# Attention backward for one query row: finer first and last loads, dK of pair 0 ahead of pair 1's K blocks, and O written out sooner

## The chip, the cores and the metric

The kernel runs on one NeuronCore of a Trainium2 chip. Its engines each run their own list of instructions in order: TensorE (PE in the profile, with PEld for its weight loads), VectorE (DVE), ScalarE (ACT), GpSimd (POOL) and SyncE (SP), which here only issues DMAs. One list of DMAs issued by SP is worked off by sixteen DMA engines; every transfer is cut over all sixteen. The metric is the device time of one execution in microseconds. The kernel before takes 647.64 us (median of 3 runs, 647.38 to 647.68).

## The reference: what is computed

Thirty-two heads, one query row each, 8192 keys, head size 128, all in bf16. The outputs are O and the gradients of q, k and v for a given dO:

```
scores = einsum('bhqd,bhkd->bhqk', q, k) * Dh**-0.5      # q [1,32,1,128], k, v [1,32,8192,128]
attn   = softmax(scores, axis=-1)
out    = einsum('bhqk,bhkd->bhqd', attn, v)
# and the vector-Jacobian product of this with grad_out: dq, dk, dv
```

With one query row, p the softmax row and dp[k] = dO . v[k], the gradients are dv[k] = p[k] dO, ds[k] = p[k] (dp[k] - sum(p dp)) scale, dq = sum over k of ds[k] k, and dk[k] = ds[k] q. So every row of K and V is read once, and every row of dK and dV written once: 134.23 MB read and 134.23 MB written.

## The kernel before

**Tiling.** The heads go in 16 pairs (`HP`), and the K or V of a pair is one tile of 128 partitions with 128 rows (slots) each, 4 MB. A tile has 8 units of 16 slots (`NU`, `CH`). There are three K buffers (`K_BUFS`, L22) and two V buffers (`V_BUFS`, L23). `load_k` (L78) and `load_v` (L82) fetch a whole tile with one DMA. The products dK and dV overwrite the K and V tile in place, and are written out from there, so a buffer can be loaded again only when its write has landed.

**What a pair needs.**
- `k_blocks` (L159): VectorE transposes a unit of K in 32x32 blocks into a buffer `XK_sb`, of which there are three.
- `k_scores` (L164): four matmuls a unit add the scores of the unit to the bank `s_ps`; `q_win` holds the weights.
- `s_back` (L175) transposes the bank back; then the softmax (L334 to L367): maximum over a partition (`mx`, `top`), across partitions through a PE transpose (L341), `nbias`, the exponential on ScalarE (L352), the sum through a matmul (L353), the reciprocal, `p_rep` (L364) and `win_p`.
- `v_transposes` (L182): TensorE transposes four 128x128 blocks of V into one of three PSUM buffers `T_ps`, ScalarE copies them out (L190). `v_scores` makes dp of them. `contract(j, "p", ...)` (L226) sums p V into `acc_p`.
- `outer(j, "dv", r)` (L248): VectorE overwrites unit r of the V tile with p x dO. It waits until `contract` has read the unit. After the last unit SP writes the tile out.
- `v_back` (L210), `pd_sum` (L272), `ds_of` (L278): VectorE brings dp back, sums p dp, and makes ds. Then `contract(j, "ds", ...)` for dq, and `outer(j, "dk", r)` for the eight units of dK.
- `gather_copy` (L236) and `gather` (L240) fold the sums of `contract` into a column of `o_all` or `dq_all`.

**Order.** The body is under a manual schedule: each engine runs its instructions in the order in which the program writes them. The loop (L300) has 17 stages. Stage j does the scores, the softmax and the V part of pair j; in between it finishes pair j-1: `v_back`, `pd_sum` and `ds_of` among the first K units, the `ds` contraction among the later ones, and the eight `dk` units around and inside the softmax of pair j, where VectorE would wait. Stage 16 has no new pair and only finishes pair 15.

**SP's list.** K0, V0, K1, V1, K2 are issued at once at the start. From there each stage j adds, in this order: dK of pair j-1, the load of V of pair j+1, dV of pair j, the load of K of pair j+2. The list is served in order: a DMA whose condition is not met holds back all behind it. A V load waits for the landing of the dV that was in its buffer, a K load for the landing of the dK that was in its buffer. In the last pair dV is written in two parts and dK in four (`PARTS`, L17).

**The start and the end.** Before the K units, the q rows are spread (`four`, L120, four copies on VectorE), transposed by TensorE into `tp_q`, and masked into `q_blk` (L132, eight operations on VectorE); `rows_bc(0, ...)`, `do_columns` and `do_window` prepare dO (L306 to L309). After the last dK unit, `result` (L290) turns `o_all` and `dq_all` into rows and writes each with a small DMA. Both use the same buffers `half` and `fin_sb`.

Of the kernel before, what the change touches and what calls it, by code (L numbers as in the profile page):

```python
# [9 lines left out]
ALU = mybir.AluOpType  # L10
# [16 lines left out]
def kernel(  # L27
# [50 lines left out]
    def load_k(j):  # L78
        Kt[j] = kpool.tile([P, NT, D], BF16, tag="K", name="Kt")
        nc.sync.dma_start(Kt[j][:], rows_of(k, j))  # L80

    def load_v(j):  # L82
        Vt[j] = vpool.tile([P, NT, D], BF16, tag="V", name="Vt")
        nc.sync.dma_start(Vt[j][:], rows_of(v, j))
# [33 lines left out]
    for w in range(NB):  # L118
        for e2 in range(2):
            nc.vector.tensor_copy(  # L120
                four[:, 2 * w + e2], rows[:, 0, :].rearrange("h (w j e) -> h w e j", w=NB, e=2)[:, w, e2:e2 + 1, :]
                .to_broadcast([H, NQ, QD]))
# [7 lines left out]
    for c in range(2 * NB):  # L130
        for t in range(2):
            nc.vector.tensor_tensor(  # L132
                q_blk[:, :, c, 2 * t:2 * t + 2], tp[:, c, t:H:2].unsqueeze(2).to_broadcast([P, HP, 2]),
                in_quad[:, 2 * t:2 * t + 2].unsqueeze(1).to_broadcast([P, HP, 2]), op=ALU.mult)

# [13 lines left out]
    dq_all = consts.tile([P, H], F32)  # L149

# [30 lines left out]
    def v_transposes(j, c):  # L181
# [4 lines left out]
        for i in range(TB):  # L186
            m = c * TB + i
            nc.tensor.transpose(T_ps[:, i, :], words[:, m * P:(m + 1) * P], ident_f[:])  # L188
        b = c % (NX // TB)
        nc.scalar.copy(XV[j][:, b * TB:(b + 1) * TB, :], T_ps[:])  # L190
# [109 lines left out]
    for j in range(HP + 1):  # L300
        p_ = j - 1
        if j < HP:
            x = st[j] = {}
            if j == 0:
                q_window(0)
                first = psT.tile([P, 512], F32, tag="T", name="first")  # L306
                rows_bc(0, first[:, 256:512])
                do_columns()
                do_window(0)  # L309
            k_blocks(j, 0)  # L310
            k_scores(j, 0)
        if j > 0:
            v_back(p_)
            pd_sum(p_)
            gather(p_, "p", st[p_]["m"])
        if j < HP:
            for u in (1, 2):
                k_blocks(j, u)
                k_scores(j, u)
        if j > 0:  # L320
            ds_of(p_)
        for u in range(3, NU):
            if j < HP:
                k_blocks(j, u)
                k_scores(j, u)
            if j > 0 and u >= 4:
                contract(p_, "ds", (u - 4) * DQ, (u - 3) * DQ)
        if j > 0:
            gather_copy("ds")
            outer(p_, "dk", 0)  # L330
        if j < HP:
            s_back(j)
        if j > 0:
            outer(p_, "dk", 1)  # L334
        if j < HP:
            mx = small.tile([P, 1], F32, tag="mx")
            nc.vector.tensor_reduce(mx[:], x["sn"], axis=AX.XY, op=ALU.max)
            top = small.tile([P, 1], F32, tag="top")
            nc.vector.tensor_scalar_mul(top[:], mx[:], scale)  # L339
            x["m"] = psM.tile([P, 512], F32, tag="m", name="m_ps")  # L340
            nc.tensor.transpose(x["m"][:, 128:256], top[:].to_broadcast([P, P]), ident_f[:])  # L341
        if j > 0:
            gather(p_, "ds", st[min(j, HP - 1)]["m"])
            outer(p_, "dk", 2)
        if j < HP:
            nbias = small.tile([P, 1], F32, tag="nbias")
            for t in range(2):
                nc.vector.tensor_reduce(nbias[t * M:(t + 1) * M, :], x["m"][t * M:(t + 1) * M, 128 + t * M:128 + (t + 1) * M],
                                        axis=AX.X, op=ALU.max, negate=True)
            e = x["e"] = small.tile([P, NT], F32, tag="e", name="e")  # L350
            rs = small.tile([P, 1], F32, tag="rs")
            nc.scalar.activation(e[:].rearrange("p (u g) -> p u g", u=NU), x["sn"], ACT.Exp, bias=nbias[:], scale=scale, accum_out=rs[:])  # L352
            nc.tensor.matmul(x["m"][:, 0:1], lhsT=ones_f[:], rhs=rs[:], start=True, stop=True,  # L353
                             skip_group_check=True)
            if j + 1 < HP:
                rows_bc(j + 1, x["m"][:, 256:512])
                q_window(j + 1)
        if j > 0:
            outer(p_, "dk", 3)
        if j < HP:  # L360
            rinv = x["rinv"] = small.tile([P, 1], F32, tag="rinv", name="rinv")
            nc.vector.reciprocal(rinv[:], x["m"][:, 0:1])
            x["p"] = small.tile([P, NT, R], BF16, tag="prep", name="p_rep")
            nc.scalar.activation(x["p"][:], e[:].unsqueeze(2).to_broadcast([P, NT, R]), ACT.Copy, scale=rinv[:])  # L364
            window("p", x["p"][:, :, 0].rearrange("p (g j) -> p g j", j=4))
            x["p_s"] = small.tile([P, NT], F32, tag="p_s", name="p_s")
            nc.vector.tensor_scalar(x["p_s"][:], e[:], rinv[:], scale, op0=ALU.mult, op1=ALU.mult)  # L367
        if j > 0:
# [4 lines left out]
        if j == HP:  # L373
            break
        for r in range(NU):
            v_transposes(j, 2 * r)
            v_transposes(j, 2 * r + 1)
# [9 lines left out]
        if j == HP - 1:  # L387
            pass

    result(o_all, out_0)  # L390
    result(dq_all, out_1)
# [31 lines left out]
```

## Time and profile before

The profiled execution took 647.51 us, 0.13 us under the median of the three runs; its span of instructions is 645.7 us, so 1.8 us lie around it.

| What | Value |
|---|---|
| Median of 3 runs | 647.64 us |
| Profiled execution / its span | 647.51 us / 645.7 us |
| SP's DMA queue | 268.46 MB, 97.3% of the sixteen engines' span |
| PE / DVE / ACT busy | 78% / 80% / 34% of the span |
| Moved over the span, read and written | 416 GB/s |
| K tile, V tile: issue to landing, median | 29.2 us, 29.0 us |
| dV tile, dK tile: issue to landing, median | 30.7 us, 22.1 us |

An engine's busy time is the time in which an instruction of its own ran; issuing DMAs does not count. The times from issue to landing include the time that a transfer stands in line behind earlier ones. The view in 40 slices has one digit or number for each 16.1 us of the span. A line of the queue's view reads: start in us, how long the issuing took or the group lasted, the queue, the line, the transfer and how many.

### The profile page before, as it was taken

The numbers are of one execution on the slowest core, as the hardware profiler recorded it, in microseconds if no ns is written. First come the engines' busy times: TensorE is split into PE (matmuls) and PEld (weight loads), VectorE is DVE, ScalarE is ACT, GpSimd is POOL, SyncE is SP. The second block draws the span as 40 slices with busy tenths as digits, with TensorE's granted clock in tenths as the row PEclk, the third lists the DMA queues.
The fourth block names the chain that finished last, engine by engine and source line by source line (L and its number), as shares of the span: only waits on it lengthen the run. The fifth ranks groups of instructions, "written<-read, shape, count | busy, mean of one in ns | idle before, by whom it ended". The sixth has DMA issues, their size and how long they took to land.

```text
span 645.7 us, 8436 instructions
## 1 busy us (share of the span) xinstructions
PE 506.6 (78%) x3480; PEld 284.4 (44%) x3480; DVE 513.9 (80%) x658; ACT 219.9 (34%) x504; POOL 3.2 (0%) x10
## 2 busy tenths in 40 slices
PE   1787888776788877689878888877788778797771
PEld 0353536353353644346345353543446345353541
DVE  3578989996788888688778788877888788787873
ACT  1241606152250524306134160522506134160430
POOL 1000000000000000000000000000000000000000
PEclk9898898986887777887678887778977679886785
DMA  9998799999999999999999999999999999999796
GB/s 385 428 422 328 287 394 431 439 422 432 431 427 431 435 427 417 439 427 429 440 425 427 445 424 427 442 427 425 439 429 427 442 427 431 437 425 430 341 435 283
DMA packets 10022, 269.01 MB, mean 417 GB/s; under 512 B 1280, under 2 KB 1280, under 8 KB 1280
## 3 DMA queue, kind: packets, MB, share of 16 engines
q1 hardware_dynamic: 9888, 268.46, 97.3%
q8 instruction: 27, 0.44, 0.3%
q14 instruction: 11, 0.09, 0.0%
q10 hardware_dynamic: 96, 0.02, 0.0%
HBM read 134.23 MB, written 134.23 MB: 416 GB/s over the span
## 4 chain that ended last, share of the span: by engine, by line
DMA 51%; PE 28%; DVE 14%; ACT 5%; issue 1%; DVEq 0%; SPq 0%; ACTq 0%
DMA Kt<-in_k_dram 29%; DMA out_dram<-Kt 21%; PE s_ps L171 13%; DVE Kt L253 6%; PE T_ps L188 5%; DVE XK_sb L161 4%; PE m_ps L245 3%; PE acc_ds L232 2%; PE acc_p L232 2%; DVE sT L178 1%; DMA out_dram<-fin_sb 1%; ACT p_rep L364 1%; ACT e L352 1%; ACT win_p L224 1%; PE dp_ps L202 1%
## 5 line engine op out<-in xcount | busy, mean ns | idle before, releaser
L171 PE MATMUL s_ps<-XK_sb,q_win 128*128 128x512 bf16 x512 | 161.5, 461 | 45.0 <-DVE XK_sb L161 44.1
L161 DVE STREAM_TRANSPOSE XK_sb<-Kt 128x1024 f32<-128x1024 f32 x128 | 150.7, 1220 | 29.3 <-DMA Kt<-in_k_dram 26.6
L253 DVE TENSOR_TENSOR Vt<-p_rep,qd 128x2048 bf16<-128x2048 bf16 x128 | 152.6, 1223 | 24.8 <-PE acc_p L232 18.6
L188 PE MATMUL T_ps<-ident_f,Vt 128*128 128x128 f32 x1024 | 171.0, 321 | 0.0
L190 ACT COPY XV_sb<-T_ps 128x512 f32<-128x512 f32 x256 | 139.1, 588 | 72.7 <-PE T_ps L188 72.2
L188 PEld LDWEIGHTS T_ps<-ident_f,Vt 128*128 128x128 f32 x1024 | 135.8, 164 | 38.1 <-issue 23.4
L253 DVE TENSOR_TENSOR Kt<-ds_rep,qd 128x2048 bf16<-128x2048 bf16 x128 | 150.6, 1211 | 1.4 <-PE acc_ds L232 0.9
L171 PEld LDWEIGHTS <-q_win 128*128 128x128 bf16 x512 | 54.5, 116 | 140.9 <-issue 117.5
L232 PE MATMUL acc_p<-Vt,win_p 128*32 128x512 bf16 x512 | 57.3, 438 | 3.3 <-ACT win_p L224 3.3
L238 ACT COPY S_ds<-acc_ds 128x512 f32<-128x512 f32 x16 | 9.4, 585 | 141.7 <-PE acc_ds L232 141.7
L202 PE MATMUL dp_ps<-XV_sb,do_win 128*32 128x512 bf16 x512 | 34.8, 385 | 12.7 <-ACT XV_sb L190 12.7
L232 PE MATMUL acc_ds<-Kt,win_ds 128*32 128x512 bf16 x512 | 40.5, 400 | 1.6 <-ACT win_ds L224 1.6
L178 DVE STREAM_TRANSPOSE sT<-s_ps 128x512 f32<-128x512 f32 x16 | 11.5, 717 | 27.4 <-PE s_ps L171 27.4
L247 ACT COPY o_all<-m_ps 128x2 f32<-128x2 f32 x16 | 2.6, 160 | 87.7 <-PE m_ps L245 87.7
L341 PE MATMUL m_ps<-ident_f,top 128*128 128x128 f32 x16 | 5.3, 330 | 28.9 <-DVE top L339 28.9
L232 PEld LDWEIGHTS <-win_p 128*32 128x32 bf16 x512 | 13.4, 94 | 30.8 <-issue 22.4
L202 PEld LDWEIGHTS <-do_win 128*32 128x32 bf16 x512 | 14.2, 94 | 28.7 <-issue 22.0
L353 PE MATMUL m_ps<-rs,ones_f 128*128 128x1 f32 x32 | 8.5, 334 | 21.9 <-ACT e L352 21.9
L245 PE MATMUL m_ps<-lane,S_p 128*128 128x2 f32 x128 | 24.7, 315 | 0.0
L245 PEld LDWEIGHTS m_ps<-lane,S_p 128*128 128x128 f32 x128 | 24.1, 280 | 0.0
L232 PEld LDWEIGHTS <-win_ds 128*32 128x32 bf16 x512 | 8.4, 97 | 28.8 <-issue 27.1
L245 PEld LDWEIGHTS m_ps<-lane,S_ds 128*128 128x128 f32 x128 | 18.5, 220 | 1.6 <-ACT S_ds L238 1.6
(59 smaller groups left out, 203.7 us busy)
## 6 DMA issues: line engine op xcount, KB each, us to landing
Kt<-in_k_dram SPq DMA_DIRECT2D x16, 4096.0 KB, 29.2
Vt<-in_v_dram SPq DMA_DIRECT2D x16, 4096.0 KB, 29.0
out_dram<-Vt SPq DMA_DIRECT2D x15, 4096.0 KB, 30.7
out_dram<-Kt SPq DMA_DIRECT2D x15, 4096.0 KB, 22.1
out_dram<-Vt SPq DMA_DIRECT2D x2, 2048.0 KB, 12.6
out_dram<-Kt SPq DMA_DIRECT2D x4, 1024.0 KB, 7.0
out_dram<-fin_sb SPq DMA_DIRECT2D x2, 8.0 KB, 4.2
rows<-in_q_dram ACTq DMA_DIRECT2D x1, 8.0 KB, 6.3
```

What stands on the lines that cost most here:

```text
L161: nc.vector.transpose(XK[j, u][:].rearrange("p g w i -> p (g w i)"), slots(Kt[j], u, NU).rearrange("p g d -> p (g d)").bitcast(F32))
L171: nc.tensor.matmul(st[j]["s"][:], lhsT=q_win[:, c, at:at + P], rhs=cols[:, c // 2, c % 2], start=(u == 0 and c == 0), stop=(u == NU - 1 an ...
L178: nc.vector.transpose(sT[:].rearrange("p g r -> p (g r)"), x["s"][:])
L188: nc.tensor.transpose(T_ps[:, i, :], words[:, m * P:(m + 1) * P], ident_f[:])
L190: nc.scalar.copy(XV[j][:, b * TB:(b + 1) * TB, :], T_ps[:])
L202: nc.tensor.matmul(out[b * QD:(b + 1) * QD, :], lhsT=do_win[:, b // 2, e2, at:at + QD], rhs=cols[:, z, e2, :, b * QD:(b + 1) * QD], start= ...
L224: nc.scalar.copy(wins[which][t * M:(t + 1) * M, :, 4 * t:4 * t + 4], src[t * M:(t + 1) * M])
L232: nc.tensor.matmul(acc[which][b * QD:(b + 1) * QD, :], lhsT=wins[which][:, g, :], rhs=X[:, 4 * g:4 * g + 4, :].rearrange("p n d -> p (n d) ...
L238: nc.scalar.copy(S[:].rearrange("p j d -> p (j d)"), acc.pop(which)[:])
L245: nc.tensor.matmul(bank[:, at:at + 2], lhsT=S[:, i, :], rhs=pick[:, i, 0:2], start=(i == 0), stop=(i == 3), skip_group_check=True)
L253: nc.vector.tensor_tensor(slots(G, r, NU).rearrange("p n (a b) -> p n a b", b=R), slots(rep, r, NU).unsqueeze(2).to_broadcast([P, CH, D // ...
L353: nc.tensor.matmul(x["m"][:, 0:1], lhsT=ones_f[:], rhs=rs[:], start=True, stop=True, skip_group_check=True)
```

## The change

1. `load_k` issues the first tile K0 in four DMAs of 1 MB, `load_v` issues V0 and V15 in four.
2. The four copies into `four` move from VectorE to ScalarE. The eight `q_blk` operations become `q_columns` and come after the first two K units of pair 0; `rows_bc(0, ...)`, `do_columns` and `do_window` come after the second unit's scores.
3. `v_transposes` is split: the transposes, and `v_copy`, the copy on ScalarE.
4. In the stages 0, 1 and 16 (`ends`) the order is another. Stage 1: after two K units, `ds_of`, then the whole `ds` contraction, all eight `dk` units with the write of dK0, and the load of V2; then the other six K units. In the softmax of the stages 0 and 1, where `dk` units no longer stand, the first four V transposes go in, and two of their copies before `p_rep`.
5. In the other stages: two more K units before `ds_of`, as before, but `gather(..., "p", ...)` after `ds_of` and no longer before those units; each quarter of the `ds` contraction one K unit earlier; the second `dk` unit before `s_back` and no longer after it; `gather(..., "ds", ...)` after `p_s` and no longer ahead of `nbias`; `rows_bc` of the next pair after that.
6. Stage 16: O's `result` follows `gather(..., "p", ...)` directly; dq's `gather` and `result` follow the sixth `dk` unit. SP's list ends with O, three quarters of dK15, dq, the last quarter.

```diff
     def load_k(j):
         Kt[j] = kpool.tile([P, NT, D], BF16, tag="K", name="Kt")
-        nc.sync.dma_start(Kt[j][:], rows_of(k, j))
+        parts = 4 if j == 0 else 1
+        for c in range(parts):
+            nc.sync.dma_start(slots(Kt[j], c, parts), rows_of(k, j, c, parts))
 
     def load_v(j):
         Vt[j] = vpool.tile([P, NT, D], BF16, tag="V", name="Vt")
-        nc.sync.dma_start(Vt[j][:], rows_of(v, j))
+        parts = 4 if j in (0, HP - 1) else 1
+        for c in range(parts):
+            nc.sync.dma_start(slots(Vt[j], c, parts), rows_of(v, j, c, parts))
...
-            nc.vector.tensor_copy(
+            nc.scalar.copy(
                 four[:, 2 * w + e2], rows[:, 0, :].rearrange("h (w j e) -> h w e j", w=NB, e=2)[:, w, e2:e2 + 1, :]
...
+    def q_columns():
+        for c in range(2 * NB):
+            for t in range(2):
+                nc.vector.tensor_tensor(
+                    q_blk[:, :, c, 2 * t:2 * t + 2], ...
...
+        st[j]["T", c] = T_ps
+
+    def v_copy(j, c):
         b = c % (NX // TB)
-        nc.scalar.copy(XV[j][:, b * TB:(b + 1) * TB, :], T_ps[:])
+        nc.scalar.copy(XV[j][:, b * TB:(b + 1) * TB, :], st[j].pop(("T", c))[:])
...
     for j in range(HP + 1):
         p_ = j - 1
+        ends = j in (0, 1, HP)
+        if j == 0:
+            k_blocks(0, 0)
+            k_blocks(0, 1)
+            q_columns()
+            q_window(0)
+        blocks(1)
         if j > 0:
             v_back(p_)
             pd_sum(p_)
-            gather(p_, "p", st[p_]["m"])
...
+        blocks(1 if ends else 2)
...
         if j > 0:
             ds_of(p_)
+            gather(p_, "p", st[p_]["m"])
+            if j == HP:
+                result(o_all, out_0)
+        if ends and j > 0:
+            contract(p_, "ds", 0, NG)
+            gather_copy("ds")
+            for r in range(NU):
+                outer(p_, "dk", r)
+                if j == HP and r == NU - 3:
+                    gather(p_, "ds", st[p_]["m"])
+                    result(dq_all, out_1)
+            if j + 1 < HP:
+                load_v(j + 1)
+        if j == HP:
+            break
+        for i in range(4):
+            blocks(1)
+            if not ends:
+                contract(p_, "ds", i * DQ, (i + 1) * DQ)
+        blocks(NU)
+        if not ends:
             gather_copy("ds")
             outer(p_, "dk", 0)
-        if j < HP:
-            s_back(j)
-        if j > 0:
             outer(p_, "dk", 1)
+        s_back(j)
...
+        if ends:
+            v_transposes(j, 0)
+            v_transposes(j, 1)
+        else:
             outer(p_, "dk", 2)
...
+        if ends:
+            v_copy(j, 0)
+            v_copy(j, 1)
+            v_transposes(j, 2)
+            v_transposes(j, 3)
+        else:
             outer(p_, "dk", 3)
...
+        if not ends:
+            gather(p_, "ds", x["m"])
+        if j + 1 < HP:
+            rows_bc(j + 1, x["m"][:, 256:512])
+            q_window(j + 1)
...
-    result(o_all, out_0)
-    result(dq_all, out_1)
```

`blocks(n)` runs `k_blocks` and `k_scores` for the next n units of the stage that are left.

## The prediction

> **What bounds the kernel now.** First the page's 40 slices and its queues. SP's queue keeps the sixteen DMA engines at work for 97.3% of the span. Only two places on the line of slices fall well below 430 GB/s: slices 4 and 5 (48 to 81 us), and the end.
>
> ```profile
> DMA  9998799999999999999999999999999999999796
> GB/s 385 428 422 328 287 394 431 439 422 432 431 427 431 435 427 417 439 427 429 440 425 427 445 424 427 442 427 425 439 429 427 442 427 431 437 425 430 341 435 283
> ```
>
> Then the busy time by stages, cut at those places (columns: window, length, busy PE, PEld, DVE, ACT, POOL, granted TensorE clock, DMA share, GB/s).
>
> ```profile
> 60.00:70.50 10.50, 8.88 (x54) 6.56 (x55) 9.34 (x13) 5.95 (x14) 0.00 (x0) 0.67 0.26 110
> 70.50:604.00 533.50, 433.99 (x2995) 242.63 (x2993) 439.56 (x553) 184.22 (x422) 0.00 (x0) 0.82 1.00 429
> 604.00:612.00 8.00, 7.57 (x40) 5.63 (x41) 7.83 (x9) 4.97 (x11) 0.00 (x0) 0.57 0.58 250
> ...
> 641.00:645.70 4.70, 0.00 (x0) 0.00 (x0) 0.00 (x0) 0.25 (x1) 0.00 (x0) 0.50 0.04 16
> ```
>
> From 70.5 to 604 the engines never rest: nothing that compute does there can shorten the run, as long as each DMA is issued before the line is empty. What can be won lies in three holes: 10.5 x 0.74 = 7.8 us at 60 to 70.5, 3.4 us at 604 to 612, and some 4 us behind 641. SP's own list says what opens the first and the last.
>
> ```profile
> 44.19 0.35 SPq L261 DMA_DIRECT2D out_dram<-Vt  x1
> 68.99 0.34 SPq L261 DMA_DIRECT2D out_dram<-Kt  x1
> 69.43 0.38 SPq L84 DMA_DIRECT2D Vt<-in_v_dram  x1
> 79.51 0.33 SPq L261 DMA_DIRECT2D out_dram<-Vt  x1
> 82.02 0.34 SPq L80 DMA_DIRECT2D Kt<-in_k_dram  x1
> 104.83 0.33 SPq L261 DMA_DIRECT2D out_dram<-Kt  x1
> ...
> 636.16 7.70 SPq L297 DMA_DIRECT2D out_dram<-fin_sb  x2
> ```
>
> Five loads and dV0 keep the line full until dV0 lands, its first of sixteen parts at 61.53 and its last at 64.34 (landing times in the trace; the engines drift apart). Then nothing is issued until dK0 at 68.99. At the end O's write goes out behind the last dK part, and dq's must wait for O's landing, because both use `fin_sb`: the third of these waits (group, total in us, times, longest); the other two come up in stage 2.
>
> ```profile
> DVE rinv L362 <- ACT qd L269: 12.5, 15, 1.7
> ...
> DVE pdt L280 <- ACT o_all L247: 10.5, 10, 1.6
> ACT fin_sb L296 <- DMA out_dram<-fin_sb: 10.0, 1, 10.0
> ```
>
> **The change part by part.** A transfer of 4 MB takes 9.7 us in a full line (first parts of K0, V0, K1, V1 land at 12.57, 22.29, 32.01, 41.70), and 10.9 us from issue to the first landing in an empty one (dK14, 610.19 to 621.13).
>
> *Start, pair 0.* K0 lands at 13.14. A quarter is 2.43 us, so the first is there at 13.14 - 3 x 2.43 = 5.9. Two K transposes at 1.2 lead to 8.3, `q_columns` 0.9 to 9.2 (7.99 to 8.85 now), `q_window` 0.26 and handovers to 9.6, against 14.46. The copies moved to ScalarE cost some 1.0 there (two alike take 0.49), beside the K transposes; with the q rows landing at 7.01 as now they would hold the scores until 9.9, no more. The scores are slower than one thinks: a unit (four matmuls) is spaced 1.7 us at half clock and 1.04 at full clock.
>
> ```profile
> 584.62 1.87 PE L171 MATMUL s_ps<-XK_sb,q_win 128*128 128x512 bf16 x4 [3.75 <-DVE XK_sb L161]
> ...
> 595.48 1.04 PE L171 MATMUL s_ps<-XK_sb,q_win 128*128 128x512 bf16 x4
> ```
>
> Two cold units take it to 13.0. Then `rows_bc`, a cast, two copies and two transposes (0.42 + 0.37 + 0.49 + 0.40 = 1.7) now stand in TensorE's list, to 14.7. Six units end at 20.9 if warm, 24.9 if cold. The clock came back 2.8 us after the first score matmul now; I take 22.0 for `sT`, against 23.52: 1.5 us gained of the 4.9.
>
> From `sT` to the last dV0 unit it is now 44.16 - 23.52 = 20.64. Four of the sixteen groups of V transposes go ahead, of which the first two ran ahead already; the other two (1.97 cold) leave the chain of contractions, and `rows_bc` and the second pair of transposes hold the first contraction by 0.75: 19.4. dV0 ends at 41.4, 2.8 earlier. It lands as now, behind K2. V0 in quarters gives nothing beyond that: at 22.9 it is in before its later blocks are asked for.
>
> *Stage 1.* Now 35.3 us (44.16 to 79.48). Up to `sT` it is 13.56, of which 1.18 is a dK unit and 1.20 a wait for scores: 11.18 stay. Added are eight dK units at once, 9.17 (pair 15's row, 626.54). Ahead of them TensorE has a unit of scores 1.0, the gather 1.0 and the first contraction 0.6, where VectorE is ready 1.7 earlier. Behind the last K transpose come 1.1 for its scores. And TensorE has nothing from the end of the contraction until the third K unit, 7 us: it comes back at half clock, and three units at 1.7 against VectorE's 1.15 cost 1.7. Sum 24.8.
>
> The Trainium skill speaks against this order too: TensorE: Matmul & The Clock Gate, Part 1, says that the clock falls to half after an idle window of about 3.4 us and returns after about as long of sustained work. By the rule two units would run cold and the extra be some 1.1; the trace is worse than the rule, for at 584 the half clock lasted 10.2 us with TensorE at work.
>
> From `sT` on, 19.4 as in stage 0 and 1.0 for dq's gather, now in front of the contractions: 20.4. The dK units that filled VectorE's idle time in the softmax are gone from there. Stage 1 becomes 45.2, ten longer, and dV1 ends at 41.4 + 45.2 = 86.6, 7.1 later than now. dK0 is issued at about 41.4 + 15.5 = 57, before the line is empty: the first hole closes. But on SP K3 stands behind dV1, and V2 lands by 81 to 84: a new hole opens there, and everything on the chain to dK1 is 7.1 late.
>
> *Stage 2 and the regular stages.* Now 25.35 from dV1's end to dK1's issue, VectorE busy for 22.31 of it. The second dK unit fills the 1.20 wait before `sT` (0.8 gained, as a quarter of the contraction now precedes the last scores), `nbias` loses the wait for `dq_all` (0.77 at this place, 0.5 counted), `rinv` the wait for `qd` (0.82, 0.6 counted): 1.9. So dK1 is issued at 86.6 + 23.45 = 110.05, against 104.83. Now, however, dK1 stood in line until K3 landed, first part 110.64, last 113.4. In the new order the line is empty and it lands 10.9 later, at 121.0, against 120.44 (first) and 123.09 (last): 0.6 lost on the first DMA engines, 2.1 won on the last ones. I take a gain of 0.8. Behind dK1 there is V3, dV2 at 86.6 + 33.4 = 120 and K4; dK2 at 143.5 comes before K4 is through (about 150): the line stays full, and the 1.9 a stage buy nothing more until the end.
>
> *The end.* Stage 15 is 1.9 shorter from K15's landing to dK14's issue. The hole at 604 shrinks by that, but only for those of the sixteen engines that run ahead; the last part of dV14 lands at 612.89, and from there at most 0.3 was to be won. V15 in quarters costs as much: the quarters of dK15 land 2.49 apart, 9.96 a tile against 9.7. (The Trainium skill, DMA: Bandwidth & Descriptors, Rules for kernel authors, puts full bandwidth at 1 MiB or more per DMA with 128 partitions; by it the quarters would be free, and the row says 0.26.) For K0 and V0 this is covered by what is late in the start anyway. In stage 16, O's transposition enters TensorE's list ahead of the contraction (0.6), but `pdt` no longer waits for `o_all` (1.1 there): even. O is written behind dV15 and lands by 633; dq follows while dK15 is still in line. The end is then the last dK quarter, at 642.98 now, instead of dq's landing at 644.89: 1.9 gained.
>
> **Sum.** 645.7 - 0.8 - 0.3 + 0.3 - 1.9 = 643.0 of span, and 1.8 around it: 644.8, against 647.51 for this execution, which lies 0.13 under the median.
>
> **Bounds.** The unshown cost is stage 1. From below: VectorE alone, 11.2 + 9.2 + 1.7, and 6.5 + 9.8 for the softmax and eight dV units, 38.4. From above: cold throughout, six units 10.2 instead of 6.9 and dV units 2.44 apart as at 29.9 to 34.7, 53. I stay nearer to stage 0 of now, which has the same bare softmax, than to either.
>
> **The rivals.** (a) Stage 1 runs at VectorE's floor. For it: the early V transposes keep TensorE at work. Against: the idle 7 us. dV1 ends at 79.8, dK1 is issued at 103.2, gain about 6.8: 638.8. (b) Slower: TensorE stays at half clock through stage 1, so dK1 is issued at 115.5 or later; 5 lost at the start, 1.9 won at the end: 650.6. It decides from dK1 at 114 on. For it: 61.68 to 68.5 is at half clock today, in this very softmax. Against: at 595 the clock came back under scores. (c) The hole only moves, and the start loses what the end wins, dK1 at 112 to 113: 647. For it: four transfers, dK0 to K3, fill 39 us, and compute had only some 4.5 us in hand at dK1.
>
> **How the numbers follow.** Mine (642 to 646.3) 0.58, (a) and what lies between 0.13, (b) 0.12, (c) 0.17. A difference under 0.2% (1.3 us) can't be told from none here. Faster 0.58 + 0.13 with little more from (c), 0.72; same 0.16; slower 0.12. The range leaves out most of (a) and of (b): 639.5 to 648.0.
>
> **What would show it.** Right: dK0 issued before 60 us and no hole at 62 to 70; dV1 at 84 to 89; a hole before dV1 and another before dK1; sums of DMA idle time nearly as now before 121; O's write before dK15's. The regular stages show dK issued earlier at equal times of the loads. Wrong: dV1 before 81 (then a), dK1 after 114 (then b), a hole later than 125, or an end that is still a write of `fin_sb`.

## The result and the profile after

The changed kernel takes 643.69 us (median of 6 runs, 641.65 to 644.92); the kernel before takes 647.88 us beside it (6 runs, 647.38 to 648.36). The ratio is 0.9934, with a 95% interval of 0.9918 to 0.9951: 4.2 us shorter. The profiled execution of the changed kernel took 644.92 us, with a span of 643.1; it is the longest of the six, 1.2 us above their median.

The same views as before, of the changed kernel. First the page's 40 slices and SP's queue (packets, MB, share of the sixteen engines' span).

```profile
DMA  8999988999999999999999999999999999999996
GB/s 365 442 431 421 423 336 360 374 438 423 427 435 429 426 429 438 419 429 439 429 428 432 439 425 427 438 431 431 429 438 428 430 436 429 431 427 427 403 416 271
...
q1 hardware_dynamic: 11184, 268.46, 97.8%
```

The dip that stood in slices 4 and 5 (328 and 287 GB/s) now fills slices 6 to 8 (336, 360, 374), and the one at 341 is 403. Idle DMA time is 2.2% of 643.1 = 14.1 us instead of 2.7% of 645.7 = 17.4. The stages (columns as before):

```profile
60.00:70.50 10.50, 7.64 (x44) 4.51 (x42) 3.96 (x9) 3.41 (x9) 0.00 (x0) 0.93 1.04 446
...
80.00:85.00 5.00, 3.60 (x38) 1.85 (x37) 4.74 (x5) 2.94 (x7) 0.00 (x0) 1.00 0.36 151
85.00:103.00 18.00, 12.66 (x86) 5.82 (x84) 17.15 (x28) 3.33 (x10) 0.00 (x0) 0.99 1.00 409
103.00:108.00 5.00, 4.85 (x26) 3.47 (x25) 4.52 (x4) 2.54 (x7) 0.00 (x0) 0.50 0.49 210
108.00:604.00 496.00, 405.43 (x2811) 231.52 (x2807) 416.19 (x518) 177.35 (x400) 0.00 (x0) 0.83 1.00 429
604.00:612.00 8.00, 7.61 (x61) 4.95 (x58) 6.23 (x6) 3.87 (x7) 0.00 (x0) 0.77 0.92 393
...
640.00:643.10 3.10, 0.00 (x0) 0.00 (x0) 0.00 (x0) 0.00 (x0) 0.00 (x0) 0.50 0.03 13
```

The hole at 60 to 70.5 (7.8 us idle) is closed. Two new ones have opened: 5.0 x 0.64 = 3.2 us before 85, and 5.0 x 0.51 = 2.6 us around 105. The hole at 604 went from 3.4 to 0.6 us. SP's list names what ends each (start in us, length of the issuing, queue, line, transfer):

```profile
37.92 0.35 SPq L269 DMA_DIRECT2D out_dram<-Vt  x1
54.54 0.34 SPq L269 DMA_DIRECT2D out_dram<-Kt  x1
64.00 0.34 SPq L88 DMA_DIRECT2D Vt<-in_v_dram  x1
83.28 0.33 SPq L269 DMA_DIRECT2D out_dram<-Vt  x1
83.70 0.38 SPq L82 DMA_DIRECT2D Kt<-in_k_dram  x1
106.41 0.33 SPq L269 DMA_DIRECT2D out_dram<-Kt  x1
...
622.70 0.34 SPq L305 DMA_DIRECT2D out_dram<-fin_sb  x1
625.26 4.87 SPq L269 DMA_DIRECT2D out_dram<-Kt  x3
632.91 0.33 SPq L305 DMA_DIRECT2D out_dram<-fin_sb  x1
633.35 0.37 SPq L269 DMA_DIRECT2D out_dram<-Kt  x1
```

dK0 goes out 14.45 us earlier than before (68.99), dV0 6.27 earlier. dV1 goes out 3.77 later, dK1 1.58 later. O's small write stands ahead of three parts of dK15, dq's ahead of the last. The wait for `fin_sb` (total, times, longest) fell from 10.0 us and lies beside transfers:

```profile
ACT fin_sb L304 <- DMA out_dram<-fin_sb: 5.1, 1, 5.1
```

The time from issue to landing, and the sixteen DMA engines, are read from the landing times in the trace. "First" and "last" are the moments at which the first and the last of the sixteen have finished their part.

| us | before | after |
|---|---|---|
| `sT` of pair 0 and of pair 1 | 23.52, 57.72 | 21.10, 63.99 |
| dK1 issued | 104.83 | 106.41 |
| dK1 landed, first / last | 120.44 / 123.09 | 117.90 / 118.52 |
| dV14 landed, first / last | 604.76 / 612.89 | 603.67 / 612.16 |
| last dK15 part landed | 642.98 | 642.20 |
| dq landed | 644.89 | before the last dK15 part |

### The profile page after: what moved, and what is told of

It is laid out like the page before. It is cut to its first block, busy times and chain, and to the rows that moved or that the text cites. A ratio compares the mean times of both kernels' runs of the same rounds, so it can differ in the third digit from the quotient of the medians.

```text
span 643.1 us, 8528 instructions
## 1 busy us (share of the span) xinstructions
PE 501.6 (78%) x3480; PEld 284.9 (44%) x3480; DVE 518.9 (81%) x654; ACT 223.2 (35%) x508; POOL 3.2 (0%) x10
## 4 chain that ended last, share of the span: by engine, by line
PE 43%; DMA 32%; DVE 18%; ACT 4%; issue 2%; ACTq 0%; SPq 0%; DVEq 0%
DMA Kt<-in_k_dram 19%; PE s_ps L176 15%; PE T_ps L193 13%; DMA out_dram<-Kt 11%; DVE XK_sb L166 5%; DVE Kt L261 5%; PE m_ps L253 4%; PE acc_p L240 4%; PE acc_ds L240 4%; ACT XV_sb L198 2%; PE dp_ps L210 2%; DMA out_dram<-fin_sb 2%; DVE Vt L261 2%; DVE sT L183 1%; DVE dpT L221 1%
## 5 line engine op out<-in xcount | busy, mean ns | idle before, releaser
L261 DVE TENSOR_TENSOR Vt<-p_rep,qd 128x2048 bf16<-128x2048 bf16 x128 | 156.4, 1225 | 63.4 <-PE acc_p L240 52.7
L176 PE MATMUL s_ps<-XK_sb,q_win 128*128 128x512 bf16 x512 | 154.3, 437 | 46.4 <-DVE XK_sb L166 41.2
L166 DVE STREAM_TRANSPOSE XK_sb<-Kt 128x1024 f32<-128x1024 f32 x128 | 151.3, 1221 | 19.3 <-DMA Kt<-in_k_dram 11.1
L176 PEld LDWEIGHTS <-q_win 128*128 128x128 bf16 x512 | 51.6, 111 | 132.0 <-issue 102.5
L232 ACT COPY win_ds<-ds 64x128 bf16<-64x128 bf16 x32 | 9.5, 296 | 79.3 <-DVE ds L291 79.1
L380 ACT ACTIVATE e<-sT,nbias 128x128 f32<-128x128 f32 x16 | 8.3, 516 | 69.9 <-DVE nbias L376 69.9
L253 PE MATMUL m_ps<-lane,S_ds 128*128 128x2 f32 x128 | 26.3, 327 | 6.1 <-DVE rinv L391 4.3
L253 PEld LDWEIGHTS m_ps<-lane,S_ds 128*128 128x128 f32 x128 | 24.9, 290 | 8.0 <-DVE rinv L391 5.5
L183 DVE STREAM_TRANSPOSE sT<-s_ps 128x512 f32<-128x512 f32 x16 | 11.5, 717 | 14.2 <-PE s_ps L176 14.2
```

Source lines behind the costliest of these rows:

```text
L166: nc.vector.transpose(XK[j, u][:].rearrange("p g w i -> p (g w i)"), slots(Kt[j], u, NU).rearrange("p g d -> p (g d)").bitcast(F32))
L176: nc.tensor.matmul(st[j]["s"][:], lhsT=q_win[:, c, at:at + P], rhs=cols[:, c // 2, c % 2], start=(u == 0 and c == 0), stop=(u == NU - 1 an ...
L183: nc.vector.transpose(sT[:].rearrange("p g r -> p (g r)"), x["s"][:])
L232: nc.scalar.copy(wins[which][t * M:(t + 1) * M, :, 4 * t:4 * t + 4], src[t * M:(t + 1) * M])
L253: nc.tensor.matmul(bank[:, at:at + 2], lhsT=S[:, i, :], rhs=pick[:, i, 0:2], start=(i == 0), stop=(i == 3), skip_group_check=True)
L261: nc.vector.tensor_tensor(slots(G, r, NU).rearrange("p n (a b) -> p n a b", b=R), slots(rep, r, NU).unsqueeze(2).to_broadcast([P, CH, D // ...
```

## The experiments

**Theories.** T: the run hangs on one chain of compute, from the first load over `sT`, dV0, stage 1 and dV1 to dK1; when dK1 is issued into an empty line, each us on that chain is a us of the run, and dK0 ahead of the K units lengthens it. Rival R1: bringing dK0 forward, so that the first hole closes, is what won the time. R2: the gain is the new end alone. R3: the quarters are only a cost. No run takes item 2 of the change (the q columns later, copies on ScalarE) by itself.

### One part of the change at a time

*The end alone.* The kernel before, with stage 16 as in the changed kernel:

```diff
+        if j == HP:
+            v_back(p_)
+            pd_sum(p_)
+            ds_of(p_)
+            gather(p_, "p", st[p_]["m"])
+            result(o_all, out_0)
+            contract(p_, "ds", 0, NG)
+            gather_copy("ds")
+            for r in range(NU):
+                outer(p_, "dk", r)
+                if r == NU - 3:
+                    gather(p_, "ds", st[p_]["m"])
+                    result(dq_all, out_1)
+            break
...
-    result(o_all, out_0)
-    result(dq_all, out_1)
```

> The kernel before with stage 16 alone in the new order: O's result right after its gather, dq's after the sixth dK unit, the whole ds contraction ahead of the dK units as before. My theory: the last write is a quarter of dK15 and no longer dq's 8 KB behind O's landing; 1.9 us shorter, 645.9. Rival, the end is set by when the last dK quarter is through and the two small writes only change places, or O's transposition delays the contraction: 647.5 to 648.

Measured: 646.17 us (645.98 to 646.5), ratio 0.9976, interval 0.9966 to 0.9985: 1.6 us. R2 explains 1.6 of 4.2.

*Two buffers for the results.* Is it the order of stage 16, or the wait for `fin_sb`? The kernel before, its order untouched:

```diff
-        half = small.tile([P, H], BF16, tag="half", name="half")
+        half = small.tile([P, H], BF16, tag="half", name="half", bufs=2)
...
-        fin_sb = small.tile([H, D], BF16, tag="fin", name="fin_sb")
+        fin_sb = small.tile([H, D], BF16, tag="fin", name="fin_sb", bufs=2)
```

> The kernel before with two buffers each for half and fin_sb, so that dq's row need not wait for O's landing; no order changed. My theory: the 1.6 us that the new end won alone is this wait; O's and dq's writes then stand together behind the last dK quarter and land with it: 646.0 to 646.3. Rival: it is the place of the writes in SP's list, ahead of dK15, that counts: 647.8.

Measured: 646.14 us (645.61 to 646.5), ratio 0.9975, interval 0.9964 to 0.9985. The end of SP's list in this kernel:

```profile
627.74 7.14 SPq L261 DMA_DIRECT2D out_dram<-Kt  x4
634.97 2.44 SPq L297 DMA_DIRECT2D out_dram<-fin_sb  x2
```

Both small writes still stand last, and the gain is the same. So the 1.6 us were dq's wait for O's landing, not the place of the writes.

*The regular stages alone.* The kernel before, with the order of the stages 1 to 15 as the changed kernel has it in 2 to 15:

```diff
-            gather(p_, "p", st[p_]["m"])
+            if j == HP:
+                gather(p_, "p", st[p_]["m"])
...
             ds_of(p_)
+            if j < HP:
+                gather(p_, "p", st[p_]["m"])
...
-            if j > 0 and u >= 4:
+            if 0 < j < HP and u < 7:
+                contract(p_, "ds", (u - 3) * DQ, (u - 2) * DQ)
...
             outer(p_, "dk", 0)
+            outer(p_, "dk", 1)
         if j < HP:
             s_back(j)
-        if j > 0:
-            outer(p_, "dk", 1)
...
-            gather(p_, "ds", st[min(j, HP - 1)]["m"])
+            if j == HP:
+                gather(p_, "ds", st[min(j, HP - 1)]["m"])
             outer(p_, "dk", 2)
...
+            if j > 0:
+                gather(p_, "ds", x["m"])
+                if j + 1 < HP:
+                    rows_bc(j + 1, x["m"][:, 256:512])
+                    q_window(j + 1)
...
```

> The kernel before with only the new order inside the stages 1 to 15 (gather of O after ds, each quarter of the ds contraction one K unit earlier, second dK unit before the scores come back, gather of dq and the next pair's rows after p_s). Start, loads and end as before. My theory: from stage 4 on the DMA engines never rest and 1.9 us less on the chain of a stage buys nothing there; in stage 1 it brings dK0 out some 1.9 us sooner, and the hole at 62 to 70 is shorter by that: 645.5 to 646.5. Rival 1: no stage that the DMA line covers counts, and the hole does not shrink either: 647.9. Rival 2: the regular stages are the real gain, about 4 us: 643.5.

Measured: 646.97 us (646.36 to 647.68), ratio 0.9987, interval 0.9978 to 0.9996: 0.8 us, less than expected. SP's list:

```profile
67.28 0.34 SPq L261 DMA_DIRECT2D out_dram<-Kt  x1
67.72 0.38 SPq L84 DMA_DIRECT2D Vt<-in_v_dram  x1
81.05 0.33 SPq L261 DMA_DIRECT2D out_dram<-Vt  x1
...
104.96 0.33 SPq L261 DMA_DIRECT2D out_dram<-Kt  x1
```

dV0 goes out at 44.10 here. dK0 comes 23.2 us behind it, 1.6 sooner than before, but dV1 comes 36.95 behind it, where it took 35.32. Part of this is the clock: here it stands at half from 60.3 to 70.5, before only from 61.7 to 68.5. The end alone and two buffers for the results, whose stage 1 has the old order, have the same 10.2 us at half clock and take 25.4 to dK0 and 36.6 to dV1. Beside them the order wins 2.2 us at dK0 and loses 0.3 at dV1. It moves work from the dK part of a stage into its V part; the stage as a whole is not shorter. That can win where dK closes a hole.

*K0 and V0 whole.* The changed kernel without the quarters at the start:

```diff
-        parts = 4 if j == 0 else 1
+        parts = 1
...
-        parts = 4 if j in (0, HP - 1) else 1
+        parts = 4 if j == HP - 1 else 1
```

> The changed kernel with K0 and V0 loaded whole, all else as changed. My theory: in the changed kernel dK1 is set by the compute chain from K0's landing on, so what the quarters won there (scores back at 21.1 in place of 23.5, dV0 written at 37.9 in place of 44.2) goes straight into dK1. Without them the first K unit starts at 13.2 and, with the two K units ahead of the q columns, the scores come back at about 25; dK1 is issued some 4 us later, at about 110.5, and the run is 2 to 4 us longer than the changed kernel, 646 to 647.6. Rival: the line of five loads hides the start (dV0 lands behind K2 in any case), the quarters do nothing: 643.7.

Measured: 651.91 us (649.1 to 652.93), ratio to the kernel before 1.0059, interval 1.0041 to 1.0076. That is 8.2 us over the changed kernel by medians, and 4.2 between the two profiled executions (649.1 and 644.92). dK1 is issued at 110.53, the 110.5 expected, 4.12 later than in the changed kernel; the time lies above the 646 to 647.6 expected. So without the quarters the change is slower than the kernel before. R3 falls for the start. Part of what the quarters are worth here comes from item 2 of the change: `sT` of pair 0 is at 27.13 without them, 2.7 to 3.6 later than in the kernels with the old start (23.52 to 24.40), which have whole loads too. The new order of the start needs the quarters. Why the median lies so much higher than the first execution is taken up below.

*Stage 1 in the regular order.* The changed kernel with

```diff
-        ends = j in (0, 1, HP)
+        ends = j in (0, HP)
```

> The changed kernel with one word taken out: stage 1 keeps the order of the regular stages (dK0's units around and inside the softmax of pair 1), while the quarters, the early V transposes of stage 0 and the new end stay. My theory: moving dK0 ahead of pair 1's K units made stage 1 ten longer (45.4 us from dV0's to dV1's write in the changed kernel, 36.5 for stage 2) and so only shifted the hole. With the regular order dK0 is issued at 37.9 + 23.2 = 61, where the line of DMAs is just about empty, dV1 at about 74, dK1 at about 97.5, before K3 is through: no hole at 80 to 85 nor at 104 to 108, first part of dK1 landed at about 111 instead of 117.9. The run gets about 5 to 7 us shorter than the changed kernel: 637 to 639. Rival 1, the early dK0 is what closed the hole: without it the hole at 62 to 70 is back, and the run is 645 or more. Rival 2, the slowest of the sixteen DMA engines sets the end and its drift takes back what the start wins: 642 to 644, as the changed kernel.

Measured: 639.75 us (637.2 to 641.19), ratio to the kernel before 0.9868, interval 0.9847 to 0.989. It is 3.9 us shorter than the changed kernel, though dK0 goes out at 63.51 and no longer at 54.54. (With `ends`, stage 1 also loses its early V transposes.) R1 falls. The stretch that was the hole at 60 to 70.5, in this kernel:

```profile
60.00:70.50 10.50, 9.86 (x70) 6.65 (x70) 8.38 (x8) 5.29 (x12) 0.00 (x0) 0.69 0.79 338
70.50:120.00 49.50, 40.56 (x295) 23.60 (x296) 42.50 (x57) 19.52 (x44) 0.00 (x0) 0.87 1.01 417
```

The run is longer than the 637 to 639 that T gave: 2.2 us of the old hole are left, and behind it there is none: dV1 goes out at 77.19 (after: 83.28) and dK1 at 100.36 (after: 106.41). The start and the regular order had already brought dK0 forward by 5.5 us; no more than some 2 us were left to be won there, and the order of stage 1 pays with two holes for it.

*Only dK0 ahead, nothing else.* The counterpart, in the kernel before:

```diff
+        if j == 1:
+            contract(p_, "ds", 0, NG)
+            gather_copy("ds")
+            for r in range(NU):
+                outer(p_, "dk", r)
+            load_v(j + 1)
         for u in range(3, NU):
...
-        if j > 0:
+        if j > 1:
             outer(p_, "dk", 1)
```

(and the quarters of the contraction and the other dK units of stage 1 taken out likewise).

> The kernel before with one part of the change: in stage 1 the whole ds contraction, the eight dK0 units, dK0's write and V2's load come after the third K unit, ahead of the other five. No quarters, no V transposes ahead, old end. My theory: dK0 is issued at about 61 and the hole at 62 to 70 closes, but stage 1 becomes some 10 us longer (45 instead of 35.3), dV1 is issued at about 89.5 and dK1 at about 115 against 104.8; dK1's first part lands at about 126 against 120.4. So the run is 3 to 5.5 us longer than before: 651 to 653. Rival, the hole was the cost and its closing the gain: 640 to 643.

Measured: 652.22 us (652.09 to 652.72), ratio 1.0068, interval 1.0056 to 1.0081: 4.4 us slower.

```profile
44.37 0.35 SPq L261 DMA_DIRECT2D out_dram<-Vt  x1
59.96 0.34 SPq L261 DMA_DIRECT2D out_dram<-Kt  x1
...
88.32 0.33 SPq L261 DMA_DIRECT2D out_dram<-Vt  x1
88.74 0.38 SPq L80 DMA_DIRECT2D Kt<-in_k_dram  x1
113.16 0.33 SPq L261 DMA_DIRECT2D out_dram<-Kt  x1
```

dK0 9.0 us sooner, and dV1 8.8 and dK1 8.3 later. Taken out of the change (3.9) or put in alone (4.4), dK0 ahead of the K units costs some 4 us.

*Without the early V transposes.* The changed kernel, with all V transposes behind the softmax:

```diff
-        if ends:
-            v_transposes(j, 0)
-            v_transposes(j, 1)
-        else:
+        if not ends:
             outer(p_, "dk", 2)
...
-        if ends:
-            v_copy(j, 0)
-            v_copy(j, 1)
-            v_transposes(j, 2)
-            v_transposes(j, 3)
-        else:
+        if not ends:
             outer(p_, "dk", 3)
...
```

> The changed kernel without the V transposes in the softmax of the stages 0 and 1: all sixteen groups stand where they stood before. My theory: with nothing else for TensorE between the scores and the contractions its clock falls to half there (as in the kernel before at 27.5 to 34.4 us; in the changed kernel it stayed full from 17.2 to 41.1), so that dV0 is written at about 41 in place of 37.9, dV1 at about 87 to 89 in place of 83.3, dK1 at 110 to 112 in place of 106.4. The run is 3 to 6 us longer than the changed kernel: 647 to 650. Rival, only the two groups that leave the chain count, 1.3 us in each stage and hidden by the line in stage 0: 644 to 645.

Measured: 650.25 us (646.95 to 652.6), ratio 1.0028, interval 1.0014 to 1.0042: 6.6 us over the changed kernel. The profiled execution is the longest of the twelve. The stretch from `sT` of pair 0 to dV0, first in this kernel, then in the changed one (window, length, PE, PEld, DVE, ACT, POOL, granted clock, DMA share, GB/s):

```profile
22.00:42.00 20.00, 16.60 (x133) 11.06 (x133) 11.65 (x15) 11.64 (x24) 0.00 (x0) 0.83 1.03 444
```

```profile
21.00:38.00 17.00, 13.66 (x134) 8.74 (x133) 11.79 (x16) 11.16 (x24) 0.00 (x0) 1.00 1.02 437
```

The same work in 20.3 us (21.80 to 42.11) instead of 16.8, at a mean clock of 0.83 instead of 1.00: in this kernel the half clock stands from 24.9 to 31.8, from the softmax into the V part, and once more from 72.7 to 79.5 in stage 1. dV0, dV1 and dK1 go out at 42.11, 90.99 and 114.14; dK1 is 7.7 us later than in the changed kernel, and later than the 110 to 112 expected.

Two effects are mixed here: the clock, and the groups of transposes that stand between the contractions again. In stage 0 most of it is the clock. A pair of transpose groups and a contraction, in this kernel at half clock, then in the changed one:

```profile
25.66 1.97 PE L193 MATMUL T_ps<-ident_f,Vt 128*128 128x128 f32 x8
27.56 0.62 PE L240 MATMUL acc_p<-Vt,win_p 128*32 128x512 bf16 x4
```

```profile
28.28 1.09 PE L193 MATMUL T_ps<-ident_f,Vt 128*128 128x128 f32 x8
29.30 0.40 PE L240 MATMUL acc_p<-Vt,win_p 128*32 128x512 bf16 x4
```

Over the stretch to 31.8 such rows add up to some 2.9 us of the 3.5 (an estimate from the rows). In stage 1 most of it is the work: from `sT` to dV1 this kernel takes 22.74, the changed one 19.29, and an execution with early transposes and as long a stretch at half clock (K0 and V0 whole, again, below: 71.8 to 78.6) takes 20.29. So there some 1.0 goes with the clock and 2.4 with the groups.

Nor do the early transposes keep the clock up every time. Eight executions have them in stage 0: four show no half clock from `sT` to dV0 (16.8 us), four show one stretch of 3.4 us (17.5 us). The six without them show 6.8 us each.

### The chain in repeated executions

Three kernels were profiled a second time, one execution each, to see what sets the difference between executions of one kernel.

*The changed kernel again.*

> The changed kernel once more, unchanged, for a second profiled execution (its times lie between 641.65 and 644.92). My theory: the time goes with the moment of dK1's issue, which the clock in the softmax of the stages 0 and 1 moves by some 2 us, and with how far the last of the sixteen DMA engines falls behind until 612. Rival: dK1's issue is the same within 0.3 us at a different time, and the spread comes from the DMA engines alone.

*K0 and V0 whole again.*

> The changed kernel with K0 and V0 whole once more, unchanged: its profiled execution, 649.1, was the shortest of six (median 651.9). My theory: in the longer executions dK1 is issued 2 to 4 us later than the 110.5 of that one, because a stretch of half clock lies in stage 0 or 1. Rival: dK1 is issued at the same time and the line is slower behind it.

*Stage 1 in the regular order again.*

> The changed kernel with stage 1 in the regular order once more, unchanged (times 637.2 to 641.19, the profiled one the longest). My theory: where stage 0 runs at full clock, dV0 is written at 37.9 and dK0 issued at 61 to 62, and the hole behind dV0 is 1 us or less in place of 3.2: 637 to 638. Rival: dK0 comes at 63.5 again.

Measured: 643.32, 651.2 and 639.56 us. The table sets each execution against the moment of its dK1, the first transfer behind the last hole of the start.

| Execution | half clock between 24 and 80 us | dV0 | dV1 | dK1 issued | time | time - dK1 |
|---|---|---|---|---|---|---|
| changed | 41.1-47.9, 51.3-61.6, 71.8-75.2 | 37.92 | 83.28 | 106.41 | 644.92 | 538.51 |
| changed, again | 39.3-46.2, 49.6-59.8, 70.1-73.5 | 36.14 | 81.52 | 104.66 | 643.32 | 538.66 |
| K0, V0 whole | 54.8-65.1, 75.3-78.7 | 43.89 | 87.39 | 110.53 | 649.1 | 538.57 |
| K0, V0 whole, again | 30.8-34.3, 54.7-65.0, 71.8-78.6 | 44.93 | 88.62 | 112.71 | 651.2 | 538.49 |
| no early V transposes | 24.9-31.8, 45.4-52.2, 55.6-65.9, 72.7-79.5 | 42.11 | 90.99 | 114.14 | 652.6 | 538.46 |

Five executions of three kernels, dK1 over 9.5 us, and the last column within 0.2 us. (dK0 alone ahead, with the old end, has 652.22 - 113.16 = 539.06.) Behind dK1 the line is full and everything takes the same time; what compute loses or gains ahead of it is the run's, one to one. T holds. It also fits that the executions of the changed kernel lie within 3.3 us and those without early V transposes within 5.7, where the kernel before holds within 1.4: before, dK1 stood in line and had slack; now nothing lies between TensorE's clock and the end. The two executions of the changed kernel part before the table's window: the first scores begin at 9.27 and 9.18, but the full clock is granted from 17.20 in the one and from 12.04 in the other, and `sT` of pair 0 comes at 21.10 and 19.37. From there to dK1 they take 85.31 and 85.29. In the two executions with whole K0 and V0, the second has one more stretch at half clock in pair 0's V part, and one twice as long in pair 1's; its dK1 is 2.18 later and its time 2.1 longer. Two executions are too few to say that the whole distance from 649.1 to the median of 651.91 is this.

The regular order of stage 1 came out at 639.56, where 637 to 638 with a hole of 1 us at most was expected. dK0 went out at 61.83; the stretch 60 to 70.5 still has a DMA share of 0.96, and the gain over its first execution is 1.6 us, for 1.7 at dK0.

### A shorter version

What is left of the hole before dK0 can be had without touching the order: write dK0 and dK1 in halves, so that the first half leaves before the last dK units are done. On top of the regular order of stage 1:

```diff
-PARTS = {("dk", -1): 4, ("dv", -1): 2}
+PARTS = {("dk", -1): 4, ("dv", -1): 2, ("dk", -16): 2, ("dk", -15): 2}
```

> The changed kernel with stage 1 in the regular order, and with dK0 and dK1 written in two halves, each as soon as its four units are done. My theory: with the regular order alone dK0 still came 2 us too late for the line (issued at 63.5, first part landed at 74.9 where a full line gives 71.7). The first half is ready some 5 us before the whole tile, at about 57 to 58, and the line stays full: dK0's second half lands at about 72 (first part), dK1 at 112 to 113, and the run is 2 to 3 us shorter than with the regular order alone: 637. Rival: the slowest of the sixteen DMA engines sets the end, and filling the hole only lets the others wait longer at 604: 639 to 640, no difference.

Measured: 638.06 us (637.1 to 638.84), ratio to the kernel before 0.985, interval 0.9837 to 0.9862. By medians that is 1.7 us shorter than without the halves, but the ranges overlap (637.2 to 641.19 there), so the times alone don't show the gain. And V15 in one DMA again:

```diff
-        parts = 4 if j in (0, HP - 1) else 1
+        parts = 4 if j == 0 else 1
```

> The same, but V15 loaded with one DMA of 4 MB again. My theory: its transposes never wait for V15 (softmax of pair 15 ends later than V15 lands), so the quarters bring nothing and cost 0.26 us of the line at most: the same time as with the halves alone within 0.5 us, or 0.3 shorter. Rival: the quarters let the last stage begin sooner, 1 us or more longer without them.

Measured: 637.52 us (636.83 to 638.38), ratio 0.984, interval 0.9827 to 0.9853. The 0.5 us against the version with quarters lie within the spread of either: the quarters of V15 bring nothing that can be seen. Its windows, where the version without halves has a DMA share of 0.79 or 0.96 from 60 to 70.5:

```profile
60.00:70.50 10.50, 10.11 (x76) 6.79 (x74) 6.94 (x6) 5.38 (x11) 0.00 (x0) 0.73 1.00 428
70.50:120.00 49.50, 40.95 (x296) 23.65 (x292) 43.12 (x57) 19.10 (x44) 0.00 (x0) 0.86 1.02 435
```

No hole is left at the start (first halves of dK0 and dK1 at 56.89 and 94.92, dV1 at 76.08). This version is 10.3 us shorter than the kernel before and 6.2 shorter than the changed one.

## Why the prediction was right, and where it was not

The forecast was 644.8 us, faster, within 639.5 to 648.0. The median is 643.69; the span of the profiled execution is 643.1, where the sum said 643.0. The places stood: the first hole closed, and new ones opened before dV1 and before dK1 because the chain through stage 1 became longer. But the closeness of the number is luck, for two errors of nearly 4 us cancel. The chain reached dK1 3.6 us sooner than in the sum, and what follows dK1 was put too low: the sum has 644.8 - 110.05 = 534.75 us from dK1's issue to the end, and the five executions of the table took 538.5. With dK1 at the predicted 110.05 that makes 648.6 (an estimate from the table), slower than the kernel before and above the stated 648.0.

- **Start.** `sT` was put at 22.0 and came at 21.10, in the second execution at 19.37; it follows the clock, which was taken to come back 2.8 us after the first score matmul and came back 7.9 and 2.9 us after it. The V part from `sT` to dV0 was put at 19.4 and took 16.8: this term was mis-sized. The early transposes were counted only as work that leaves the chain (1.97 less, 0.75 more); that the half clock shrinks with them, from 6.8 us to none here, was not counted. The run without them has 20.3 at a clock of 0.83. dV0 came at 37.92 instead of 41.4.
- **Stage 1.** Put at 45.2, it took 45.36. Up to `sT` 26.07 (24.8 predicted), from there 19.3 (20.4). The idle 7 us of TensorE and its return at half clock are there, in the groups of TensorE and VectorE (start, length, engine, line, operation, tiles, count, idle before and its releaser):

```profile
55.73 8.23 PE L176 MATMUL s_ps<-XK_sb,q_win 128*128 128x512 bf16 x24 [7.56 <-DVE XK_sb L166]
```

```profile
45.35 9.17 DVE L261 TENSOR_TENSOR Kt<-ds_rep,qd 128x2048 bf16<-128x2048 bf16 x8 [3.00 <-PE acc_ds L240]
54.44 4.62 DVE L166 STREAM_TRANSPOSE XK_sb<-Kt 128x1024 f32<-128x1024 f32 x4
...
63.99 0.72 DVE L183 STREAM_TRANSPOSE sT<-s_ps 128x512 f32<-128x512 f32 x1 [1.71 <-PE s_ps L176]
```

  TensorE was idle for 7.56 us (7 predicted), and the six K units took 63.99 - 54.44 = 9.55 (6.9 + 1.1 + 1.7 = 9.7 predicted). What was too small is the wait ahead of the first dK unit: 3.00 us, where 1.7 had been counted; that is the 1.3 by which `sT` came late. The half clock from 41.1 to 47.9 lies there: the unit of scores takes 1.86 and the gather 1.70, where 1.0 each had been counted.
- **Signs.** dK0 at 54.54 (before 60), a hole before each of dV1 and dK1, O's write ahead of dK15's: as said. Two were missed: dV1 at 83.28 lies under the 84 to 89, and the DMA idle time up to 121 us is not nearly as before (a share of 0.95 instead of 0.92, some 3 us less). dV1 came 3.3 earlier than its 86.6, and dK1 3.6 earlier than its 110.05, nearly all of it dV0's error of 3.5: stage 2 up to dK1 took 23.13, for 23.45.
- **dK1's landing.** Predicted was 0.6 lost on the first DMA engine and 2.1 won on the last; measured are 2.5 and 4.6 won (117.90 and 118.52, for 120.44 and 123.09). Of the 4.6, 0.7 are left when dV14 lands (612.16 for 612.89), and 0.8 at the last dK part. The step took what is won at dK1 as won at the end. dK1 also landed 11.5 (first) to 12.1 us (last) behind its issue, where 10.9 was taken from dK14. The line behind it, however, took 1.5 us longer for the first engine (603.67 - 117.90 = 485.8, before 484.3), and the sixteen, 0.62 apart at dK1, were 8.5 apart at 612 (8.1 before). So two errors cancelled: dK1 came 3.6 sooner than predicted, and the line behind it gave the surplus back. That is why the predicted 0.8 of gain was found at the end.
- **Regular stages.** "Stage 2 33.4" was wrong: from dV1 to dV2 the changed kernel takes 36.5, and the order alone, beside executions with as much half clock, makes the dK part 2.2 shorter and the stage 0.3 longer. dV2 came at 119.80 for the predicted 120 only because dV1 was 3.3 early. Nothing hung on it, the line being full there.
- **End.** 1.9 predicted; 1.6 with the end alone. The quarters of V15 were put at 0.3 lost and as much won; taking them out gives 0.5 us, which can't be told from none.
- **The rivals.** (a), stage 1 at VectorE's floor, did not happen: 45.4, not 38.4. (b) and (c) had their condition at dK1, 114 and 112 to 113: the changed kernel stayed under both (106.41). Its version without early V transposes had dK1 at 114.14 and that execution took 652.6, but not by (b)'s mechanism: in stage 1 the clock was at full from 52.2 to 55.6, from 65.9 to 72.7 and from 79.5 on. The second execution with whole first loads had (c)'s dK1, 112.71, and took 651.2, where (c) said 647: 4 us too low, the error of the sum once more.

What the parts are worth, each by its own run: the new end 1.6, the regular order 0.8, the early V transposes 6.6, the quarters at the start 8.2 by medians (4.2 between the profiled executions), dK0 ahead of the K units -4. They don't add up to the whole, since the first two count from the kernel before and the others from the changed one, where the chain has no slack.

## What to carry to other kernels

A hole in the transfers is closed by making its chain of compute shorter, or by writing out in smaller parts; work that is moved ahead to close it makes whatever stood behind it late, and here that cost 4 us, while writing in halves filled the old hole without it. See which transfer first meets an empty line: up to there each us of compute is a us of the run, clock included, and behind it none is. A few transposes placed in a stretch where TensorE would rest won here in two ways that were not wholly parted: work left the chain, and the stretch at half clock became shorter.

## What the runs showed of the hardware

- **The clock and short gaps.** All stretches at half clock in the table are multiples of 3.41 us long to within 0.1. In stage 1 TensorE restarts at 55.73 and is granted the full clock at 61.57, 5.8 us later. The Trainium skill, TensorE: Matmul & The Clock Gate, Part 1, describes a free-running window of 3413 ns over which activity is judged; the lengths agree, and 5.8 us lie between one and two windows. The page also says that the start of the full clock varies from run to run with the phase of the window; here the full clock comes 7.9 us behind the first score matmul in one execution of the changed kernel, which is more than two windows, and 2.9 in the other, and dK1 lies 1.75 us apart.
- **The sixteen DMA engines drift.** In the changed kernel they are 2.2 us apart at K2's landing (54.20), 0.7 behind the hole at 85, 0.62 behind the one at dK1, and 8.5 at 612; the last of them ends the run. A hole sets them level and the drift starts anew. It follows that a hole costs less than its length where the engines were apart, and closing it wins less; no run tests this by itself.
- **Behind a hole the rate stays low for a while.** In the changed kernel:

```profile
108.00:140.00 32.00, 25.93 (x193) 13.76 (x189) 27.27 (x36) 10.91 (x25) 0.00 (x0) 0.87 1.01 408
```

  and in the kernel before, behind its hole and then a stage later:

```profile
72.00:104.00 32.00, 25.86 (x196) 14.54 (x189) 27.88 (x38) 11.29 (x27) 0.00 (x0) 0.89 1.01 409
104.00:136.00 32.00, 25.47 (x204) 13.84 (x202) 29.36 (x39) 11.71 (x29) 0.00 (x0) 0.96 1.00 431
```

  The DMA engines are busy all the time and move 408 and 409 GB/s behind a hole, 431 without one. Over 32 us that is 32 x (1 - 408/431) = 1.7 us, about the 1.5 by which the first engine's way from dK1 to dV14 grew. In the regular order of stage 1, the second execution moved 413 GB/s from 70.5 to 120 behind a rest of 0.4 us of the hole, and the best version 435 in the same stretch (the halves of dK0 and dK1 are another difference between these two). That the sixteen, set level, disturb each other when they change between reading and writing together is only argued; no run here separates it.
- **A small DMA beside large packets lands later.** The q rows land 3.4 us after their issue instead of 6.3, when the first loads beside them go in packets of 8 KB (0.31 us each) instead of 32 KB (1.21 us).
